# Clearing the zero rows of eight weight buffers on POOL in place of ScalarE copies, in a two-layer attention and MLP kernel

## The chip, the cores and the metric

The kernel runs on one core of a Trainium2 chip. The metric is the device time of one execution in microseconds (us). Before the change the median of three runs is 1509.63 us (1508.83 to 1510.06). The engines are named as the profile names them: PE is TensorE (PEld its weight loads), DVE is VectorE, ACT is ScalarE, POOL is GpSimd, and SP is SyncE, which issues all DMAs of this kernel.

## The reference

The input x has 2048 tokens of width 448. The program is two equal layers, each an attention with a recurrent memory followed by a gated MLP:

```python
def _A_ref(x, mem0, Wq, Wk, Wv, Wo, seg_len):      # 16 heads of 256, segments of 32, 8 memory rows
    mem = mem0
    for s in range(n_seg):
        h = concatenate([mem, x[:, s*32:(s+1)*32]])
        q, k, v = h @ Wq, h @ Wk, h @ Wv
        p = softmax(where(mask, q k^T * scale, -1e9))
        o = (p v) @ Wo
        mem = o[:, :8]                               # goes to the next segment
        outs.append(o[:, 8:])
def _B_ref(x, W_gate, W_up, W_down):
    gate = x @ W_gate
    return (relu(gate) * (x @ W_up)) @ W_down
x = x + _A_ref(_layernorm(x), mem0, ...)
x = x + _B_ref(_layernorm(x), ...)
x = x + _A_ref(_layernorm(x), mem0, ...)             # same weights again
x = x + _B_ref(_layernorm(x), ...)
```

All data are bfloat16. The two layers share all weights.

## The kernel before

The kernel first folds the attention weights. For each head it forms A = Wq Wk^T (scaled) and B = Wv Wo, both 448 wide, so that the 64 steps of the recurrence and all tokens use A and B and never q, k, v. For this it loads Wq, Wk and Wv in pieces of 512 columns (two heads) into 16 staging buffers `Wst`, each 128 partitions by 4 blocks by 512. Buffers 0 to 7 hold Wq and Wk in four groups (the even groups in 0 to 3, the odd ones in 4 to 7); buffers 8 to 15 hold Wv. Buffers 0 to 11 lie in `Bsb`, 12 to 15 in `glu`, and these are the names that the profile shows.

A weight has 448 rows: three blocks of 128 and one of 64. The fourth block of a staging buffer is therefore half filled, and its other half must be zero, since PE transposes whole blocks of 128 x 128 (`transposes`, profile line L745, eight matmuls for one head of one buffer). In buffers 0 to 7 the zero part is partitions 64 to 127, 512 columns. In buffers 8 to 15 it is two pieces of 64 partitions x 256 columns. The zeros are written once, in `constants`: by DVE for buffers 0 to 3 (L664), and for buffers 4 to 15 by ACT, which copies from a cleared tile `hG` (L666, which the profile shows under the helper's line L441). That is 4 copies of 64x512 and 16 of 64x256.

After a transpose, ACT or DVE evicts the block from PSUM into one of seven buffers `WT` (in `glu`; 128x896, lines L441 on ACT and L444 on DVE). Then `product` (L758) multiplies transposed Wq with transposed Wk, and the result goes to `A` (L441 on ACT, L443 on DVE). For a group PE transposes the first heads of four buffers, does 28 matmuls of products, and then the same for the second heads. In the first group the load of each buffer is split into halves (L706), so that the first heads arrive before the second ones. Later loads into the same buffers wait until PE has transposed the old contents.

Nothing of this is issued in program order. `_Sched` records every operation with its engine, a cost and its dependencies, and builds the order of each engine by simulating them: an engine takes, among the operations that can start at once, the one with the lowest step and priority. Each engine then works strictly in its order and waits on semaphores. Two things are fixed beside that. PE's order is written out by hand in the string `LINE`. And where PE would idle in the plan, `filler` puts in matmuls that compute nothing (L1403); at the very start PE also runs 17 matmuls on zeros (L657). POOL operations with the flag `cross` wait for POOL's own operation before and are waited for by the next one.

SP issues the weight loads, the loads of x (`X`), the first memory rows (`PTx`, ten small DMAs after POOL's memset L865), and later all else, also in one fixed order.

Of the kernel before, what the change touches and what calls it, by code (L numbers as in the profile page):

```python
# [423 lines left out]
def ev_cost(n, src="psum", fast=False):  # L424
    return {"act": 170 + 0.833 * n, "dve": 149 + (0.53 if fast else 1.04) * n, "pool": 170 + 1.0 * n}
# [10 lines left out]
def copy_any(out, in_, scale=None):  # L436

    def fn(E, eng):
        i = in_() if callable(in_) else in_
        if eng == "act":  # L440
            return E.activation(out, i, ACT.Copy, scale=1.0 if scale is None else scale)  # L441
        if scale is not None:
            return E.tensor_scalar(out, i, scale, None, op0=ALU.mult)  # L443
        return E.tensor_copy(out, i)  # L444
    return fn
# [66 lines left out]
class _Kernel:  # L512
# [124 lines left out]
    def constants(self):  # L637
        s = self.s
        iv = self.X[4][:, 0:256].bitcast(dt.int32)
        fv = self.X[5][:, 0:256].bitcast(F32)  # L640
        s.alias[("X", 4)] = ["ci"]
        s.alias[("X", 5)] = ["cf", "cf2"]

        def pool(fn, **k):
            s.add("pool", 500, lambda E, e: fn(E), **k)

        def dve(fn, **k):
            s.add("dve", 250, lambda E, e: fn(E), **k)

        hG = self.hG[0].rearrange("p a b -> p (a b)")  # L650
        hk = [("hG", 0, q) for q in range(2)]
        s.add("dve", 400, lambda E, e: E.memset(hG[:, 0:576], 0.0), w=hk)
        wb = self.bank("C")

        def spin(E, e):
            for _ in range(17):
                i = E.matmul(wb.ap()[:, 0:D], lhsT=hG[:, 0:128], rhs=hG[:, 128:576], start=True, stop=True)  # L657
            return i
        s.add("pe", 17 * 378, spin, r=hk, w=[wb], alloc=[wb])
        for i in range(16):  # L660
            for n, (rows, cols) in enumerate([(slice(64, 128), slice(0, 512))] if i < 8 else [(slice(64, 128), slice(0, 256)), (slice(0, 64), slice(256, 512))]):
                to, of = self.Wst[i][rows, 3, cols], hG[rows, cols]
                if i < 4:
                    s.add("dve", 300, lambda E, e, to=to: E.memset(to, 0.0), w=[("Wz", i, n)])  # L664
                else:
                    s.add("act", ev_cost(cols.stop - cols.start)["act"], copy_any(to, of), r=hk, w=[("Wz", i, n)])  # L666
        pool(lambda E: E.iota(iv[:, :], [[1, 128]], base=0, channel_multiplier=-1), w=["ci"])
        dve(lambda E: E.tensor_copy(fv[:, :], iv[:, :]), r=["ci"], w=["cf"])
        dve(lambda E: E.tensor_scalar(self.ident[:, :], fv[:, :], 0.0, None, op0=ALU.is_equal), r=["cf"], w=["ident"])
        dve(lambda E: E.memset(self.maskb[:, :], 0.0), w=["mask"])  # L670
        for b in range(4):
            q = slice(32 * b, 32 * b + 32)
            dve(lambda E, q=q, b=b: E.tensor_scalar(self.maskb[q, 0:SEG], fv[q, 0:SEG], -32.0 * b, FAR, op0=ALU.is_gt, op1=ALU.mult),
                r=["cf"], w=["mask"])

        dve(lambda E: E.tensor_reduce(fv[:, 0:32], self.ident[:, :].rearrange("p (j i) -> p i j", j=4), AX.X, ALU.add), r=["ident", "mask"], w=["cf"])
        dve(lambda E: E.tensor_copy(self.Sel[:, :], fv[:, 0:32]), r=["cf"], w=["Sel"])

        mb = self.bank("C")
        for o in range(4):  # L680
            dve(lambda E, o=o: E.tensor_copy(self.Usb[:, 128 * o:128 * o + 128].rearrange("p (h q) -> p h q", h=H),
                                             self.ident[:, 8 * o:8 * o + 8].unsqueeze(1).to_broadcast([128, H, 8])),
                r=["ident"], w=[("Usb", o)])
            s.add("pe", 30, lambda E, e, o=o: E.matmul(mb.ap()[:, L * o:L * o + L], lhsT=self.Usb[:, 128 * o:128 * o + 128],
                                                       rhs=self.maskb[:, :], start=True, stop=True),
                  r=[("Usb", o), "mask"], w=[mb], alloc=[mb] if o == 0 else ())
        dve(lambda E: E.tensor_copy(self.mask8[:, :, :], mb.ap()[:, 0:4 * L].rearrange("p (o k) -> p o k", o=4)), r=[mb], w=["mask8"])
        pool(lambda E: E.memset(self.Pr[:, :], 0.0), w=[("r", "P")])
        dve(lambda E: E.memset(self.cvec[:, 0:1], EPS), w=["cvec"])
        pool(lambda E: E.memset(self.YTm[:, :, :], 0.0), w=[("YTm", c) for c in range(2)] + [("YTr", c) for c in range(2)])  # L690
        pool(lambda E: E.memset(self.Pm[:, :], 0.0), w=[("m", "P")])
        for i in range(2):
            pool(lambda E, i=i: E.memset(self.xn[i][:, KZ:KT], 0.0), w=[("xnz", i)])
        pool(lambda E: E.memset(self.Usb[:, :], 0.0), w=[("Usb", r) for r in range(4)])
        pool(lambda E: E.memset(self.uT[:, 3], 0.0), w=[("uT2", a, b) for a in range(2) for b in range(2)])
        pool(lambda E: E.memset(self.mT[:, :, :], 0.0), w=MEM + ["mTr", "mT3"])
        for i in range(2):
            pool(lambda E, i=i: E.memset(self.Px[i][:, :, :], 0.0), w=[("Px", i)])
        for l in range(2):
            for i in range(NB[l]):  # L700
                for p in range(2):
                    pool(lambda E, l=l, i=i, p=p: E.memset(self.HR[l][i][p][:, KZ:KW], 0.0),
                         w=[k for h in range(2) for k in (("HRx", l, i, p, h), *(("HRm", l, 4 * i + 2 * p + h, v) for v in range(4)))])

    def dma(self, dst, src, nbytes, r=(), w=(), prio=None, land=None):
        return self.s.add("sp", 750 if nbytes < 8192 else 640, lambda E, e: E.dma_start(dst, src), r=r, w=w, dma=nbytes, prio=prio, land=land)  # L706
# [821 lines left out]
```

## Time and profile before

| | us |
|---|---|
| median of 3 runs | 1509.63 |
| range of the runs | 1508.83 to 1510.06 |
| the profiled execution: time | 1508.01 |
| the profiled execution: span of the trace | 1506.2 |
| PE busy in the span | 1489.1 (99%) |
| DVE busy | 1147.8 (76%) |
| ACT busy | 914.4 (61%) |
| POOL busy | 166.2 (11%) |

Times in the trace count from the start of the span; the execution's own time is 1.8 us longer. A row of the timeline has start, duration, engine, line, operation, what is written and read, the count, and in brackets how long the engine stood idle before and what ended that. A helper records most copies, so one line can stand for many tiles. "PE busy" says little by itself, as matmuls are pipelined; the granted clock (1.00 is full speed) and the waits say more.

### The profile page before, as it was taken

How to read it: one execution, taken by the hardware profiler on the slowest of the kernel's cores; microseconds unless marked ns; L12 is line 12 of the kernel's file. 1: busy time of each engine (PE TensorE's matmuls, PEld its weight loads, DVE VectorE, ACT ScalarE, POOL GpSimd, SP SyncE). 2: the span in 40 equal slices, each digit the busy share in tenths (PEclk: the TensorE clock that was granted, in tenths of full speed). 3: DMA queues.
4: the chain of work that ended last, by engine and by line, in shares of the span. 5: the costliest groups of instructions: out<-in, count | busy, mean ns of one | idle time of the engine just before them, and what ended most of it. 6: DMA issues, size and time to landing. Idle time of an engine off the chain costs nothing.

```text
span 1506.2 us, 83238 instructions
## 1 busy us (share of the span) xinstructions
PE 1489.1 (99%) x37022; PEld 1058.8 (70%) x37022; DVE 1147.8 (76%) x3561; ACT 914.4 (61%) x2535; POOL 166.2 (11%) x648
## 2 busy tenths in 40 slices
PE   8999999999999999999999999999999999999999
PEld 5657566666767777677768677677768776677776
DVE  5767678787877887787877877788787788787864
ACT  7776566665655666566665666556565566565643
POOL 1010111111111111010101111011110011010000
PEclk9999999999999999999999999999999999999999
DMA  6702100000000000000000000000000000000000
GB/s 194 219 24 67 52 8 12 11 9 8 9 4 9 14 8 14 4 16 6 14 8 9 14 9 15 3 17 6 18 5 8 13 9 14 5 8 8 12 8 12
DMA packets 62582, 34.12 MB, mean 23 GB/s; under 512 B 31872, under 2 KB 62096, under 8 KB 62224
## 3 DMA queue, kind: packets, MB, share of 16 engines
q1 hardware_dynamic: 62224, 28.80, 7.3%
q8 instruction: 292, 4.78, 1.3%
q14 instruction: 66, 0.54, 0.1%
HBM read 21.36 MB, written 1.84 MB: 15 GB/s over the span
## 4 chain that ended last, share of the span: by engine, by line
PE 95%; DVE 3%; ACT 2%; issue 0%; POOL 0%; DVEq 0%
PE psG L451 24%; PE psG L1271 17%; PE psG L1369 12%; PE psC L970 11%; PE psC L931 9%; PE psG L931 3%; PE psG L1182 3%; PE psG L758 3%; PE psG L1297 3%; PE psC L451 2%; PE psC L1182 1%; PE psC L1125 1%; PE psG L745 1%; PE psG L1185 1%; PE psC L1271 1%; PE psG L970 1%
## 5 line engine op out<-in xcount | busy, mean ns | idle before, releaser
L1271 PE MATMUL psG<-HT,A 64*128 64x128 bf16 x4968 | 285.3, 216 | 0.1
L451 PE MATMUL psG<-Bsb,YT 128*128 128x448 bf16 x1288 | 276.6, 352 | 0.0
L1271 PE MATMUL psG<-HX,A 64*128 64x128 bf16 x3726 | 266.6, 216 | 0.0
L1271 PEld LDWEIGHTS psG<-HT,A 64*128 64x128 bf16 x4968 | 233.8, 94 | 14.1 <-issue 5.7
L441 ACT ACTIVATE Ug<-psG 64x128 bf16<-64x128 f32 (+2 forms) x428 | 153.6, 378 | 67.9 <-PE psG L1271 59.0
L1271 PEld LDWEIGHTS psG<-HX,A 64*128 64x128 bf16 x3726 | 193.7, 94 | 0.4 <-issue 0.4
L1369 PE MATMUL psG<-G,glu 64*128 64x128 bf16 x5936 | 187.9, 216 | 0.4 <-DVE G L444 0.2
L1369 PEld LDWEIGHTS psG<-G,glu 64*128 64x128 bf16 x5936 | 174.1, 94 | 12.5 <-issue 5.7
L970 PE MATMUL psC<-Bsb,YTm 128*32 128x448 bf16 x3584 | 181.4, 353 | 1.0 <-DVE YTm L444 0.6
L451 PEld LDWEIGHTS psG<-Bsb,YT 128*128 128x128 bf16 x1288 | 112.5, 97 | 89.3 <-issue 5.9
L931 PE MATMUL psC<-A,mT 64*32 64x448 bf16 x3948 | 154.9, 350 | 1.4 <-ACT mT L441 0.5
L1109 DVE STREAM_TRANSPOSE uT<-Usb 128x384 bf16<-128x384 bf16 x280 | 154.0, 551 | 0.9
L931 PE MATMUL psG<-A,mT 64*32 64x448 bf16 x3892 | 152.2, 350 | 0.0
L970 PEld LDWEIGHTS psC<-Bsb,YTm 128*32 128x32 bf16 x3584 | 90.0, 97 | 73.3 <-DVE YTm L444 3.1
L441 ACT ACTIVATE YT<-psG 128x448 bf16<-128x448 f32 x238 | 120.6, 543 | 11.3 <-PE psG L1185 10.4
L444 DVE CAST Ug<-psG 64x128 bf16<-64x128 f32 (+2 forms) x274 | 112.8, 422 | 18.2 <-PE psG L1271 14.3
L931 PEld LDWEIGHTS psC<-A,mT 64*32 64x32 bf16 x3948 | 79.6, 92 | 58.2 <-ACT mT L441 5.9
L1374 ACT ACTIVATE hG<-psG 128x512 bf16<-128x512 f32 (+1 forms) x126 | 68.5, 544 | 65.3 <-PE psG L1369 61.4
L451 PE MATMUL psG<-glu,hG 128*128 128x448 bf16 x448 | 98.6, 352 | 0.0
L1375 DVE TENSOR_TENSOR hG<-hG,psG 128x512 bf16<-128x512 bf16 (+1 forms) x117 | 70.6, 609 | 32.6 <-ACT hG L1374 31.7
L976 ACT ACTIVATE Ohi<-psC 128x448 bf16<-128x448 f32 x66 | 35.9, 544 | 95.6 <-PE psC L970 94.2
L931 PEld LDWEIGHTS psG<-A,mT 64*32 64x32 bf16 x3892 | 79.8, 92 | 17.4 <-ACT mT L441 0.6
(241 smaller groups left out, 2891.1 us busy)
## 6 DMA issues: line engine op xcount, KB each, us to landing
HR<-xn SPq DMA_DIRECT2D x128, 32.0 KB
Tsb<-Rsb SPq DMA_DIRECT2D x256, 1.5 KB
Tsb<-Rsb SPq DMA_DIRECT2D x256, 2.0 KB
Bsb<-in_A_Wq_dram SPq DMA_DIRECT2D x6, 384.0 KB
Bsb<-in_A_Wk_dram SPq DMA_DIRECT2D x6, 384.0 KB
HR<-Rsb SPq DMA_DIRECT2D x126, 1.5 KB
HR<-Rsb SPq DMA_DIRECT2D x126, 2.0 KB
X<-in_A_x_dram SPq DMA_DIRECT2D x16, 112.0 KB
```

Of the source, the lines that this page charges most:

```text
L441: return E.activation(out, i, ACT.Copy, scale=1.0 if scale is None else scale)
L444: return E.tensor_copy(out, i)
L451: return E.matmul(out, lhsT=lhsT, rhs=rhs, **k)
L758: i = E.matmul(bk.ap()[row0:row0 + mn, 0:D], lhsT=lhs[:, et, m0:m0 + mn], rhs=rhs[:, et, :], start=(et == 0), stop=(et == 1), tile_positio ...
L931: i = E.matmul(ub[v].ap()[32 * j:32 * j + 32, 0:D], lhsT=self.mT[rw, WHERE[b], first:first + 32], rhs=cols, start=(b == 0), stop=(b == 6), ...
L970: x = E.matmul(bo.ap()[32 * j:32 * j + 32, 0:D], lhsT=self.YTm[:, q, :], rhs=self.Bsb[:, chunks[q], :], start=(i == 0), stop=(i == 13), ti ...
L1109: self.s.add("dve", 578, lambda E, e, out=out, hh=hh: E.transpose(out, heads[hh]), r=[("Usb", 2 * half + v) for v in range(2)], w=[f"uT{ha ...
L1182: return E.matmul(ps[:, n * q:n * q + n], lhsT=HR[rows, 128 * q:128 * q + 128], rhs=PT, start=True, stop=True, tile_position=(b, 0))
L1271: i = E.matmul(ub[v].ap()[:, 128 * n:128 * n + 128], lhsT=self.A[rw, b, a0:a0 + 128], rhs=HT[rw, WHOLE[b], :, 0:SEG] if CROSS[b] is None e ...
L1369: i_ = E.matmul(two[v].ap()[:, 128 * c:128 * c + 128], lhsT=self.Wgu[rw, b, f0:f0 + 128], rhs=G[rw, WHOLE[b] if CROSS[b] is None else 4 + ...
L1374: s.add("act", 170 + 0.833 * N, lambda E, e, dst=dst, z=two[0], N=N: E.activation(dst, z.ap()[:, 0:N], ACT.Relu), r=[two[0]], w=[("hG", i, ...
L1375: s.add("dve", dv_cost(N), lambda E, e, z=two[1], N=N, dst=dst: E.tensor_tensor(dst, dst, z.ap()[:, 0:N], ALU.mult), r=[two[1]], w=[("hG", ...
```

## The change

ACT's sixteen copies of 64x256, which clear buffers 8 to 15, are no longer made. In their place POOL clears the same pieces with sixteen memsets. These are recorded last in `constants`, behind POOL's other memsets there, each with the flag `cross`. Buffers 0 to 7 are cleared as before (DVE for 0 to 3, ACT for 4 to 7).

```diff
+        rest = []
         for i in range(16):
             for n, (rows, cols) in enumerate([(slice(64, 128), slice(0, 512))] if i < 8 else [(slice(64, 128), slice(0, 256)), (slice(0, 64), slice(256, 512))]):
                 to, of = self.Wst[i][rows, 3, cols], hG[rows, cols]
                 if i < 4:
                     s.add("dve", 300, lambda E, e, to=to: E.memset(to, 0.0), w=[("Wz", i, n)])
+                elif i < 8:
+                    s.add("act", ev_cost(cols.stop - cols.start)["act"], copy_any(to, of), r=hk, w=[("Wz", i, n)])
                 else:
-                    s.add("act", ev_cost(cols.stop - cols.start)["act"], copy_any(to, of), r=hk, w=[("Wz", i, n)])
+                    rest.append(lambda to=to, i=i, n=n: s.add("pool", 350, lambda E, e, to=to: E.memset(to, 0.0), w=[("Wz", i, n)], cross=True, at=10 + n))
...
+        for f in rest:
+            f()
```

In the built program the order of PE, DVE and SP is the same, instruction by instruction. ACT has the sixteen copies less and is otherwise in the same order. POOL has the sixteen memsets between the memsets of `HR` (L702) and that of `PTx` (L865), and is otherwise in the same order.

## The prediction

> **What bounds the kernel now.** I read the page first (the chain that ended last, by engine), then the waits of TensorE (PE), then the timeline of the first 45 us by engine, because the change touches only the set-up.
>
> ```profile
> PE 95%; DVE 3%; ACT 2%; issue 0%; POOL 0%; DVEq 0%
> ```
>
> ```profile
> PE psG L758 <- ACT glu L441: 4.3, 2, 4.1
> PE psC L451 <- DVE Olo L979: 1.4, 3, 0.6
> ```
>
> The first fence is the page: 95% of the chain is PE, whose order is fixed by hand. The second is the waits of PE over the whole span (us in all, times, longest). A saving on PE's stream should therefore reach the end of the run, and the largest wait that PE has anywhere, 4.1 us at once, is for ScalarE's (ACT's) eviction of a transposed weight. The timeline of ACT, PE, DVE and SP's queue shows where it is (start, us, instruction, idle before it):
>
> ```profile
> 2.02 5.56 ACT L441 ACTIVATE Bsb<-hG 64x512 bf16<-64x512 bf16 x12
> 7.61 3.48 ACT L441 ACTIVATE glu<-hG 64x256 bf16<-64x256 bf16 x8
> 11.00 1.70 ACT L441 ACTIVATE glu<-psG 128x896 bf16<-128x896 bf16 x2
> ```
>
> ```profile
> 6.05 2.26 PE L745 MATMUL psG<-ident,Bsb 128*128 128x128 bf16 x32
> 8.15 0.61 PE L1403 MATMUL psC<-ident 128*128 128x128 bf16 x8
> 12.84 1.71 PE L758 MATMUL psG<-glu 128*64 128x448 bf16 x8 [4.08 <-ACT glu L441]
> ```
>
> ```profile
> 8.35 0.62 DVE L444 COPY glu<-psG 128x896 bf16<-128x896 bf16 x1 [0.58 <-PE psG L745]
> ```
>
> ACT copies zeros without a pause from 2.02 to 11.0 us and only then evicts two of the four transposed blocks that PE made between 6.05 and 8.3. DVE's two were done at 8.35 + 0.62 = 8.97. So PE stands from 8.76 to 12.84, and the only cause is ACT's queue of zero copies. What follows on PE, in the chain of waits (start, us, what):
>
> ```profile
> 14.54 0.75 PE psC L1403 x6
> 15.29 1.71 PE psG L745 x16
> 17.00 2.60 PE psG L758 x19
> 19.60 1.01 PE psG L745 x16
> 20.61 0.02 issue
> 20.63 0.64 DVE glu L444
> 21.27 0.04 issue
> 21.31 2.46 PE psG L758 x24
> ```
>
> Sixteen transposes (L745) take 1.71 us here and 1.01 us a little later: the pause is paid for twice. The table by windows (length, busy of PE, PEld, DVE, ACT and POOL, then granted clock, DMA share, GB/s) shows why:
>
> ```profile
> 11.20:11.40 0.20, 0.00 (x0) 0.00 (x0) 0.00 (x0) 0.20 (x1) 0.00 (x0) 0.82 0.40 113
> 18.00:18.20 0.20, 0.20 (x4) 0.15 (x2) 0.00 (x0) 0.20 (x1) 0.00 (x0) 0.61 0.23 77
> 7.92:11.33 3.41, 0.84 (x15) 0.66 (x12) 0.62 (x1) 3.24 (x9) 0.00 (x0) 1.00 0.71 200
> 11.33:14.74 3.41, 1.91 (x11) 0.91 (x12) 0.16 (x1) 1.91 (x3) 0.00 (x0) 0.50 0.85 247
> 14.74:18.15 3.41, 3.41 (x30) 2.63 (x29) 1.09 (x2) 1.14 (x2) 0.00 (x0) 0.50 0.93 290
> ```
>
> The clock falls from 1.00 to 0.50 at about 11.33 (0.82 is the mean of that slice) and returns at about 18.15.
>
> **The change part by part.** *ACT.* Sixteen zero copies of 64x256 leave; four of 64x512 stay. Eight cost 3.48, or 0.435 each; the row of twelve (four large, eight small) leaves 5.56 - 3.48 = 2.08 for the large ones, so ACT is free at 4.1 instead of 11.0. Its two evictions (1.70 / 2 = 0.85 each) then start as the first and third blocks come, and end by about 8.8, before DVE's second at 8.97. That copy is late next: from a copy's start to PE's the chain shows 0.64 + 0.04 (20.63 to 21.31), so PE starts L758 at 8.35 + 0.68 = 9.03. Gain at this point: 12.84 - 9.03 = 3.81.
>
> *The clock.* PE's pause falls from 4.08 to about 0.3 us, so I take the clock to stay at 1.00. Then, by full-speed rows: eight L758 at 2.46 / 24 each are 0.82 (to 9.85), six fillers L1403 at 0.61 / 8 each 0.46 (to 10.31).
>
> *A load is late next.* The following transposes need the second half of a third weight buffer, the seventh load that SP issues. SP does not wait for anybody here, so this load does not come earlier:
>
> ```profile
> 4.20 1.13 SPq L706 DMA_DIRECT2D Bsb<-in_A_Wk_dram  x2
> 5.37 1.13 SPq L706 DMA_DIRECT2D Bsb<-in_A_Wq_dram  x2
> 6.54 1.14 SPq L706 DMA_DIRECT2D Bsb<-in_A_Wk_dram  x2
> 7.72 1.13 SPq L706 DMA_DIRECT2D Bsb<-in_A_Wq_dram  x2
> ```
>
> ```profile
> 7.24 0.90 PEld L745 LDWEIGHTS psG<-ident,Bsb 128*128 128x128 bf16 x16 [0.31 <-DMA Bsb<-in_A_Wk_dram]
> ```
>
> The fourth load, issued at 4.20, released PE's weight load at 7.24, 3.04 later. The seventh, issued at 7.72, would release it at 10.76, and the matmul about 0.1 behind: 10.85. So PE waits some 0.5 us for DMA. From there at full speed: 16 transposes 1.01, twenty L758 2.05, 16 transposes 1.01, and 0.70 from 20.61 to 21.31: the L758 that started at 21.31 starts at 15.62. **Sum: 21.31 - 15.62 = 5.7 us.** With no wait for that load it would be 6.2.
>
> *Behind that.* The order of PE, DVE and SP is untouched, and the loads of the next group wait on SP for PE's transposes, so they move forward with PE. The four loads of the second group, which wait for nobody, do not move; the last ends at about 18.0 (in the slice from 18.00 the DMA share falls to 0.23). Its transposes are in
>
> ```profile
> 25.30 1.71 PE L745 MATMUL psG<-ident,Bsb 128*128 128x128 bf16 x24
> ```
>
> and would come at 25.30 - 5.7 = 19.6: a margin of 1.6 us. I keep 5.7 to the end of the run.
>
> *POOL.* Sixteen memsets of 64x256, each waiting for POOL's own instruction before, stand between the HR and PTx memsets (POOL's timeline, and SP's row for the first user of PTx):
>
> ```profile
> 4.17 0.64 POOL L698 MEMSET Px<- 128x256 bf16 x2
> 4.76 2.24 POOL L702 MEMSET HR<- 128x192 bf16 x10
> 6.95 0.31 POOL L865 MEMSET PTx<- 128x256 bf16 x1
> ...
> 63.07 0.64 POOL L444 COPY uT<-tl 64x128 bf16<-64x128 bf16 x2 [1.36 <-DVE tl L1102]
> ```
>
> ```profile
> 25.12 2.23 SPq L706 DMA_DIRECT2D PTx<-in_A_mem_dram  x6
> ```
>
> Unwaited memsets cost 0.22 (HR) to 0.32 (Px); two waiting copies add about 0.06 between them (0.64 for two of 0.29). I take 0.40: 6.4 us, from 7.0 to 13.4, and PTx's memset ends at 13.8. SP's DMA into PTx, at 25.12 - 5.7 = 19.4, waits for it, with SP's later loads behind it. So POOL costs nothing up to (19.4 - 0.4 - 7.0) / 16 = 0.75 each. The cleared buffers hold the value weights, which are not even asked for until
>
> ```profile
> 34.42 1.12 SPq L706 DMA_DIRECT2D Bsb<-in_A_Wv_dram  x2
> ```
>
> *DVE beside POOL.* The trace shows the same short copy at 0.57 and at 0.22, both beside memsets of POOL:
>
> ```profile
> 3.16 0.57 DVE L681 COPY Usb<-ident 128x128 bf16<-128x128 bf16 x1
> ...
> 5.35 0.22 DVE L681 COPY Usb<-ident 128x128 bf16<-128x128 bf16 x1
> ```
>
> So each of DVE's evictions from 7 to 13 us could cost 0 to 0.35 more. On the path lie the copies that end at 8.97; two of them cost 0.7 at most, of which the wait for the load hides 0.5. I take 0 and keep 0.2 for the range. The Trainium skill, "SBUF — State Buffer", section "Who interferes with whom", has DVE and GpSimd exclude each other only where DVE works in a two-port mode or reads two SBUF operands; an eviction from PSUM is neither, and by it the term is 0 too. No row of this trace shows such an eviction wholly beside a memset.
>
> The profiled execution took 1508.01 us, 1.6 below the median of 1509.63 shown; on it the change gives 1502.3, on the median **1503.9**.
>
> **The rivals.**
>
> *The clock falls all the same.* The window from 7.92 to 11.33 had 0.84 us of PE and the clock fell at its end; in the changed kernel it would hold 0.84 + 0.82 + 0.46 + 0.5 = 2.6 of 3.41. For it: 1.91 of 3.41 did not bring the clock back. Against: it is three times as full as the window that lost it. If it falls for one such window, half of 3.41 is lost, 1.7 us: 1505.6; for two, 1507.3. The Trainium skill, "TensorE: Matmul & The Clock Gate", Part 1, describes a free-running window of about 3.4 us that grants or takes the clock by activity. The trace agrees on the length: 18.15 - 11.33 is twice 3.41. Part 4 adds that transposes do not count as activity in the same way; by that the window would hold only 1.9 of 3.41, which no row here can exclude.
>
> *The gain is taken up later* by transfers that cannot start sooner. From 14.74 to 18.15 the DMA share is 0.93, and the next loads would join that queue at once. If they cost PE half the gain, 1506.8. Against: no DMA is among PE's longer waits.
>
> *Nothing is gained:* if PE's real wait at 12.84 were for something else. ACT ran without a gap up to its release, so I hardly believe it: 1509.6.
>
> *Slower: POOL holds up SP.* If clearing 64 partitions at a time is dear on POOL, PTx's memset comes late, and SP's DMA into PTx stands in front of the loads of the fourth group. It passes today's place of 25.12 from (25.12 - 0.4 - 7.0) / 16 = 1.1 us a memset. At 1.6 each it would end at 33.0, 7.9 later than today; if none of that is slack, 1517.5. Against: the short memsets of the trace cost 0.32 or less, on 128 partitions.
>
> **How the numbers follow.** Forecast as summed: 0.70, with 1503.2 to 1504.9 as its own range (0.5 for the load, 0.2 for DVE, and the 1.2 us that the three runs of before are apart). Clock falls: 0.11. Gain taken up: 0.10. Nothing: 0.05. Slower: 0.04. A measurement here tells about 0.2%, or 3 us: faster means below 1506.6. The first case, most of the second and half of the third are faster: 0.85; within 0.2%: 0.11; slower: 0.04. The range goes from 1502.8 (all loads in time, 6.2, less run spread) to 1506.8, which takes in both middle cases.
>
> **What would show it.** ACT's evictions start before 7 us; the first L758 starts near 9.0; the granted clock is 1.00 from 7.9 to 18.2; PE waits about 0.5 for Wq at 10.8; the L758 row of 21.31 stands near 15.6; POOL's memsets end by 14; the same shift of 5.7 at 60 us and at the end. Wrong, if the clock dips, if a DMA wait over 1 us appears on PE before 45 us, or if the shift shrinks between 60 us and the end.

## The result, and the profile after

| | before | after |
|---|---|---|
| median of the runs on the same chip, us | 1508.83 (1507.65 to 1510.23, 9 runs) | 1504.3 (1503.03 to 1506.16, 9 runs) |
| ratio of the times, 95% interval | | 0.9972 (0.9961 to 0.9982) |
| profiled execution: time, span, us | 1508.01, 1506.2 | 1504.3, 1501.8 |
| mean granted clock of TensorE | 0.998 | 1.000 |

The forecast was 1503.9 us, 5.7 below the median it started from. The kernel became faster by 4.5 us against the runs beside it. A second comparison (first experiment) gives 5.5.

First the waits of TensorE over the whole span of the changed kernel (us in all, times, longest):

```profile
PE psC L451 <- DVE Olo L984: 1.4, 3, 0.6
PE psC L657 <- DVE hG L652: 1.2, 1, 1.2
PE psG L763 <- DVE glu L444: 1.0, 4, 0.3
```

The wait of 4.1 us for ScalarE, the largest before, is no longer among them. Every wait over 0.3 us that is left was there before (the one for DVE's evictions has grown from 0.7 to 1.0 us in all), and a wait of 0.2 us for a weight load is new. (Lines from 706 on stand 5 further down in this kernel: L745 is now L750, L758 is L763, L1403 is L1408, L706 is L711.)

The timeline of the first 35 us of the changed kernel, by engine (start, us, instruction, idle before it):

```profile
2.03 2.18 ACT L441 ACTIVATE Bsb<-hG 64x512 bf16<-64x512 bf16 x4
7.37 1.81 ACT L441 ACTIVATE glu<-psG 128x896 bf16<-128x896 bf16 x2 [3.17 <-PE psG L750]
```

```profile
7.07 2.85 POOL L669 MEMSET Bsb<- 64x256 bf16 x8
9.97 2.85 POOL L669 MEMSET glu<- 64x256 bf16 x8
12.88 0.32 POOL L870 MEMSET PTx<- 128x256 bf16 x1
```

```profile
7.82 0.62 DVE L444 COPY glu<-psG 128x896 bf16<-128x896 bf16 x1 [1.61 <-PE psG L750]
8.71 0.62 DVE L444 COPY glu<-psG 128x896 bf16<-128x896 bf16 x1 [0.27 <-PE psG L750]
```

```profile
1.22 5.67 PE L657 MATMUL psC<-hG 128*128 128x448 bf16 x17 [1.22 <-DVE hG L652]
6.73 1.95 PE L750 MATMUL psG<-ident,Bsb 128*128 128x128 bf16 x32
8.51 0.61 PE L1408 MATMUL psC<-ident 128*128 128x128 bf16 x8
9.39 0.95 PE L763 MATMUL psG<-glu 128*64 128x448 bf16 x8 [0.27 <-DVE glu L444]
10.27 0.51 PE L1408 MATMUL psC<-ident 128*128 128x128 bf16 x6
10.96 1.07 PE L750 MATMUL psG<-ident,Bsb 128*128 128x128 bf16 x16 [0.18 <-DMA Bsb<-in_A_Wq_dram]
```

ScalarE stands idle for 3.17 us before its first eviction, so it is no longer what is late. POOL clears the sixteen halves while PE transposes. DVE's copies take 0.62 beside these memsets, as they did without them. PE starts L763 at 9.39 where it started at 12.84. After these products and six fillers it waits 0.18 us for the weight load, to 10.96. The chain that ended last, from there on (start, us, what):

```profile
8.35 2.56 DMA Bsb<-in_A_Wq_dram
...
10.96 1.07 PE psG L750 x16
12.02 2.01 PE psG L763 x20
14.04 1.01 PE psG L750 x16
...
15.75 2.46 PE psG L763 x24
```

The sixteen transposes that took 1.71 us take 1.07, and the L763 that started at 21.31 starts at 15.75: 5.56 us earlier. The part up to this row is called the head below. The same three windows as before (length, busy of PE, PEld, DVE, ACT and POOL with their counts, then granted clock, DMA share, GB/s):

```profile
7.92:11.33 3.41, 2.96 (x43) 2.11 (x41) 1.78 (x3) 1.81 (x3) 2.89 (x10) 1.00 0.74 200
11.33:14.74 3.41, 3.41 (x47) 2.34 (x45) 1.87 (x3) 2.67 (x5) 1.58 (x6) 1.00 0.85 251
14.74:18.15 3.41, 3.14 (x39) 1.85 (x36) 1.87 (x3) 2.17 (x4) 0.00 (x0) 1.00 1.02 298
```

The clock stays at 1.00 in all three, where it was 0.50 in the last two.

How the shift (start of a matmul in the first trace of before less its start in the other trace, matmuls taken in order, median of 15; times are those of before) goes on behind the head, with three further executions that the experiments gave:

| at, us | 22 | 60 | 650 | 990 | 1200 | end |
|---|---|---|---|---|---|---|
| after | 5.56 | 5.55 | 5.9 | 6.2 | 5.3 | 4.44 |
| after, second execution | 5.55 | 5.25 | 4.9 | 4.7 | 4.5 | 4.74 |
| after with two loads exchanged | 5.53 | 5.03 | 5.6 | 5.9 | 5.9 | 6.01 |
| before, second execution | 0.90 | 0.90 | 1.8 | 2.2 | 1.8 | 1.54 |

Behind 60 us it moves by -1.1 to +1.0 in steps of 0.2 to 0.4, and it moves as much between two executions of the kernel before. One step, at 995 us (-0.30), is the same in the first row and in the last, so that one belongs to the first trace of before.

### The profile page after: what moved, and what is told of

The parts are those of the page before. It is cut to its first block, busy times and chain, and to the rows that moved or that the text cites. A ratio compares the mean times of both kernels' runs of the same rounds, so it can differ in the third digit from the quotient of the medians.

```text
span 1501.8 us, 83238 instructions
## 1 busy us (share of the span) xinstructions
PE 1487.6 (99%) x37022; PEld 1057.6 (70%) x37022; DVE 1148.6 (76%) x3561; ACT 908.3 (60%) x2519; POOL 171.8 (11%) x664
## 4 chain that ended last, share of the span: by engine, by line
PE 95%; DVE 3%; ACT 1%; SPq 0%; issue 0%; DMA 0%; POOL 0%; DVEq 0%
PE psG L451 24%; PE psG L1276 17%; PE psG L1374 12%; PE psC L975 11%; PE psC L936 9%; PE psG L936 3%; PE psG L1187 3%; PE psG L763 3%; PE psG L1302 3%; PE psC L451 2%; PE psC L1187 1%; PE psC L1130 1%; PE psG L750 1%; PE psG L1190 1%; PE psC L1276 1%; PE psG L975 1%
```

## The experiments

The theory: the ScalarE queue is the wait; the gain is a shorter pause plus a clock that no longer falls, cut off by the next weight load; nothing behind the head belongs to the change. The rivals: the clock term is worth nothing by the end; POOL has a price that shows only later; the pause is not ScalarE's.

**1. The changed kernel again.** Same code, to see which steps behind the head recur.

> The changed kernel once more, for a second trace. In the first one the head of the kernel is 5.56 us earlier than in the profile of before, and the end 4.44 us. If the missing 1.1 us are scatter of single executions (short stops of PE at places that differ from run to run), a second trace shows the head within 0.2 us of the first one and the end anywhere from 4 to 6 us ahead, with the steps between 60 us and the end at other places. If the change itself loses the 1.1 us further on, the steps stand at the same places again (near 995, 1032, 1167, 1334 to 1390 and 1468 us). Time: 1503 to 1506.

It took 1504.29 us (1503.27 to 1506.69, 5 runs), ratio 0.9968 (0.9955 to 0.9981), beside a before of 1509.75 (1507.48 to 1512.23, 23 runs). The end of the head and the clock are the same; at 17.9 us one eviction of ScalarE came late for PE and took 0.3 off the shift. The steps behind 60 us stand at other places and sizes than in the first execution (second row of the table). I therefore take the loss of 1.1 us behind 60 us in the first trace as scatter of single executions; a small true loss inside that scatter isn't excluded, since the shift shrank in both traces (5.55 to 4.44 and 5.25 to 4.74).

The head of this execution tests the terms of the forecast better than the first one. The 17 opening matmuls took 5.05 us, nearly as in the first trace of before (4.99), and its timeline reads

```profile
9.14 0.95 PE L763 MATMUL psG<-glu 128*64 128x448 bf16 x8 [0.27 <-DVE glu L444]
10.96 1.07 PE L750 MATMUL psG<-ident,Bsb 128*128 128x128 bf16 x16 [0.43 <-DMA Bsb<-in_A_Wq_dram]
```

PE comes 0.25 us sooner than in the first execution and waits that much longer: the load lets it go at 10.96 in both.

**2. The pause filled, ScalarE's work left as it was.** Kernel before, with 58 more filler matmuls in PE's pause, so that only the clock is changed.

```diff
 # filler(), for the first filler only
+        self.nf = getattr(self, 'nf', 0) + 1
+        if self.nf == 1:
+            n += 58
```

> The kernel before with 58 more idle matmuls of PE (L1403) in its pause behind the first transposes, so that the pause lasts under 1 us, while ACT's zero copies and all else stay. My theory: the first L758 still starts at about 12.8 (it waits for ACT), but the clock stays at 1.00, and the L758 that started at 21.31 starts at 12.84 + 0.82 + 0.46 + 1.01 + 2.05 + 1.01 + 0.70 = 18.9: 2.4 us gained, 1507 for a median of 1509. The rival, that the slow stretch behind the pause comes from loads or evictions and not from the clock: it stays at 21.3 and the time at 1509.

The chain shows the clock term as expected, at the head:

```profile
12.84 0.95 PE psG L761 x8
13.79 0.44 PE psC L1406 x6
14.23 0.89 PE psG L748 x16
```

The eight L761 took 0.95 where they took 1.71 at half clock, the first L761 of the 24 starts 2.45 us earlier than before, and the granted clock is 1.000. But the kernel took 1511.83 us (1510.39 to 1513.17, 10 runs), ratio 1.0013 (1.0003 to 1.0022): slower. The profiled execution was the slowest of the ten. Its span of 1511.4 ends 5.2 later than before's, so 7.6 us went behind the head in it; by the medians, 2.1 apart, it is about 4. The waits of PE name no engine for it:

```profile
PE psG L934 <- issue: 2.3, 4, 1.1
PE psG L1274 <- issue: 2.0, 4, 0.8
```

"issue" is time in which the engine waited for nothing that the profile shows. The largest such stop is a piece of the chain at 134.69:

```profile
134.69 1.14 issue
```

So the run told two things at once, and its total tells nothing of the clock. Two more kernels (5 and 9) take them apart.

**3 and 4. Smaller doses.** The changed kernel with four, then six, of the eight buffers given back to ScalarE.

```diff
-                elif i < 8:
+                elif i < 12:     # dose 8: POOL clears buffers 12 to 15
+                elif i < 14:     # dose 4: POOL clears buffers 14 and 15
```

> Half of the change: POOL clears buffers 12 to 15 only (eight memsets), ACT keeps the eight copies into Bsb. ACT would be free at 7.6, evicts from 7.6 to 9.3, and PE's first L758 starts at 9.45, nearly as in the changed kernel (9.39 there), because DVE's second copy ends at 9.3 anyway; then the load holds PE to 10.9. So the whole gain with half of the change: within 0.3 us of the changed kernel at 16 us, 1504 to 1505. The rival, that ACT's freed time counts by the copy (7 us of copies for 5.6 us of gain): half the gain, 2.8 us, 1506 to 1507.

> A quarter of the change: POOL clears buffers 14 and 15 only (four memsets). ACT is free at 11.0 - 4 x 0.435 = 9.3, evicts to 11.0, the first L758 starts at 11.1, and PE pauses 2.3 us. The load is no longer waited for. If a pause of this length leaves the clock at 1.00, the L758 of 15.75 starts at 17.1, a gain of 4.2 against before: 1505 for 1509. If the clock falls, one window of 3.41 us costs 1.7 and two 2.5 as in before: 18.8 to 19.6, 1506.5 to 1507.3. The half dose beside it says whether the gain falls off only here.

With eight halves moved: 1505.76 us (1504.02 to 1507.27, 7 runs), ratio 0.9974 (0.9963 to 0.9984); 1504 to 1505 was expected. The shift at the head is 5.38, nearly that of all sixteen: beyond eight, ScalarE is not what is late. Then a load of the second group is, in the chain:

```profile
13.04 6.12 DMA Bsb<-in_A_Wq_dram
...
19.25 0.61 PE psG L750 x8
```

The transposes came at the load, and the shift at 60 us is 4.46. PE waits 0.9 us for this load here and 0.4 in run 6; in the changed kernel its transposes start at 18.14 without a wait.

With four halves moved: 1507.07 us (1505.75 to 1509.01, 10 runs), ratio 0.9984 (0.9975 to 0.9994). The pause is half as long, and the clock holds at 1.00 (timeline, windows and chain of this kernel):

```profile
11.09 0.95 PE L763 MATMUL psG<-glu 128*64 128x448 bf16 x8 [2.01 <-ACT glu L441]
```

```profile
7.52:10.94 3.42, 1.51 (x24) 1.34 (x24) 0.68 (x2) 3.32 (x7) 1.14 (x4) 1.00 0.72 194
```

```profile
17.10 2.46 PE psG L763 x24
```

PE starts L763 at 11.09 for 12.84, 1.75 earlier, but the head's shift is 21.31 - 17.10 = 4.21: the other 2.46 is the clock, as in run 2 (2.45). A window with 1.51 us of PE in 3.42 kept it, the one with 0.84 in 3.41 lost it. Both hold the eight fillers (0.61), and the rest is transposes. That fits transposes counting as activity, but these two windows don't prove it: the pause was also shorter (2.01 for 4.08). Run 7 has a window that does: from 44.05 to 47.46 (its windows counted in steps of 3.41 from the rise of its clock at 6.50) PE was busy for 2.15 us, 2.01 of them transposes (the row is of these alone), and the clock stayed at 1.00:

```profile
44.05:47.46 3.41, 2.01 (x32) 1.66 (x30) 1.00 0.87 253
```

Without its transposes it would have held 0.14 us, less than any window here that lost the clock, and stood empty from 44.05 to 46.80.

On this chip the medians gain 2.7, 4.0 and 5.5 us with 4, 8 and 16 halves moved, for 4.21, 5.38 and 5.56 at the head. The order is that of the heads, though the intervals overlap. The two small doses have 1.4 to 1.5 less at the end. The wait for the load explains a part for eight (0.9), and stops of PE put down to issue another: they come to 1.3 us in the trace with four, 0.8 with eight and 0.3 with sixteen. The rest is open.

**5. The place in the stream alone.** Kernel before, with the 17 opening matmuls of 448 columns cut into 75 of 102: 58 instructions more, the same columns, nothing else.

```diff
-            for _ in range(17):
-                i = E.matmul(wb.ap()[:, 0:D], lhsT=hG[:, 0:128], rhs=hG[:, 128:576], start=True, stop=True)
+            for _ in range(75):
+                i = E.matmul(wb.ap()[:, 0:102], lhsT=hG[:, 0:128], rhs=hG[:, 128:230], start=True, stop=True)
```

> A control for the fillers. With 58 more idle matmuls the head was 2.45 us earlier and the end 5.2 us later than before: 7.6 us went in stops of PE behind 60 us, which the profile puts down to issue. Here the kernel before gets the same 58 more matmuls without any time: the first spin on zeros (L657) is 75 matmuls of 102 columns in place of 17 of 448 (7650 columns for 7616). If the place of PE's later instructions in its stream is what makes the stops, the head is as before (L758 at 12.8 and 21.3) and the end 6 to 8 us later than before, with stops at the same matmuls as with the fillers: 1515 to 1517. If the stops came from the fillers or from the time at which the rest runs, the time is that of before, 1509 to 1510.

It took 1511.74 us (1510.23 to 1512.75, 7 runs) beside a before of 1508.2 (1505.69 to 1509.44, 19 runs), ratio 1.0024 (1.0013 to 1.0035). At the head it is 0.23 behind, at the end 3.7: 3.5 us were lost between, again to

```profile
PE psG L1271 <- issue: 0.9, 2, 0.6
PE psG L931 <- issue: 0.8, 1, 0.8
```

The stops stand at the same matmuls of before's order as in run 2 for a part: at 135.7 us (-1.13 here, -1.50 there), 387.8 (-0.48, -0.46), 938.3 (-0.55, -0.55), 1303.3 (-0.44, -0.80). Others of run 2, at 116.2 and 323.1, have none here. The loss was half of what was expected.

**6. Two loads exchanged.** The changed kernel with SP's fifth and seventh load exchanged, so that the load PE waits for at 10.96 comes 2.3 us sooner.

```diff
+        sp = [k for k, o in enumerate(seq) if o.eng == "sp"]
+        for k in (8, 9):
+            p, q = sp[k], sp[k + 4]
+            seq[p], seq[q] = seq[q], seq[p]
+            seq[p].seq, seq[q].seq = p, q
```

> The changed kernel with two loads of SP exchanged: the second half of the third buffer is issued fifth in place of seventh (and that of the first buffer seventh). PE's wait for a load at 10.9 goes; its transposes start when the six fillers end, near 10.8, and the L758 of 15.75 starts at 15.5 to 15.6. The load of 12.4 (third buffer of the second group), for which PE waited 0 to 0.9 us in three traces, is then next to hold it, at about 18. So 0 to 0.2 us in all: the same as the changed kernel within what can be measured. The rival, that the seventh load cost more than the 0.2 us of the trace: over 0.5 us at 16 us.

It took 1502.92 us (1501.96 to 1505.95, 7 runs), ratio 0.997 (0.9959 to 0.9981): not told apart from the changed kernel. At the head nothing is won (5.53), but this doesn't show what the load is worth: the 17 opening matmuls took 6.04 us in this execution (5.67 in the changed kernel's first), and PE came to the transposes only at 11.00, without a wait. PE then waits for a load of the second group to 18.68, as with eight halves.

**7. POOL made late.** The changed kernel with eleven more memsets of 128x1792 on POOL between the sixteen and PTx's, to put a number on the rival "slower".

```diff
+        for i in range(11):
+            s.add("pool", 61, lambda E, e: E.memset(self.YTm[:, :, :], 0.0), cross=True, at=10,
+                  w=[(k, c) for k in ("YTm", "YTr") for c in range(2)] if i == 10 else [])
```

> The changed kernel with eleven more memsets of 128x1792 on POOL between the sixteen and that of PTx; they clear again what is zero already. They cost 1.65 each, 18 us, so PTx's memset ends near 31.4 in place of 13.2, and SP's DMA into PTx, at 20.7 in the changed kernel, waits about 10.7 us, with the loads of the fourth group behind it (25.15 to 33.8). My theory: cover is worth what the loads have in hand. The first of them is needed at 35.5 and would be there at about 37.3, the others a little later: 2 to 4 us lost, 1506 to 1508. If all of the delay reaches PE: 8.5 us, 1513. If nothing does: 1504.

It took 1509.12 us (1508.81 to 1511.25, 10 runs), ratio to before 1.0013 (1.0003 to 1.0022). Timelines of POOL and of SP's queue:

```profile
12.88 18.11 POOL L710 MEMSET YTm<- 128x1792 bf16 x11
31.04 0.31 POOL L873 MEMSET PTx<- 128x256 bf16 x1
```

```profile
31.38 2.06 SPq L714 DMA_DIRECT2D PTx<-in_A_mem_dram  x6
33.48 0.93 SPq L714 DMA_DIRECT2D Bsb<-in_A_Wk_dram  x2
```

In the changed kernel, without the eleven, the same queue reads

```profile
20.68 2.23 SPq L711 DMA_DIRECT2D PTx<-in_A_mem_dram  x6
25.15 0.93 SPq L711 DMA_DIRECT2D Bsb<-in_A_Wk_dram  x2
```

The shift is 5.59 at 22 us and 5.35 at 30. SP then stands at PTx's DMA 10.7 us longer, the loads queued behind it come late, and between 30 and 50 us the shift falls from 5.35 to -0.73: 6.1 us, more than expected. The rival's mechanism is real. Its deciding point was put too low: here the DMA is issued 6.3 us later than in the kernel before (31.38 against 25.12) and PE loses 0.7 to before, so some 5.5 us of that are slack. The sixteen memsets would have to fill POOL from 7.07 to about 31, 1.5 us each, before the gain is gone; they take 0.36.

**8. The kernel before again**, one execution.

> The kernel before once more, for a second trace, to see how much two executions of one kernel differ behind the head: steps of 0.1 to 0.4 us at some twenty places if the scatter is that of single executions, the head the same within 0.1 us if the clock falls and rises at the same distance from PE's pause. The clock's windows need not stand at the same times, so the slow stretch could be one window long in place of two: then the L758 of 21.3 stands near 20.

One execution, 1506.46 us, span 1504.7. The windows, of 3.41 us, stand elsewhere:

```profile
9.80:13.21 3.41, 0.37 (x4) 0.31 (x6) 0.00 (x0) 2.85 (x5) 0.00 (x0) 1.00 0.77 221
13.21:16.62 3.41, 3.41 (x31) 2.50 (x26) 0.63 (x1) 1.30 (x2) 0.00 (x0) 0.50 0.89 275
16.62:18.00 1.38, 1.38 (x17) 0.85 (x18) 1.03 (x2) 0.73 (x3) 0.00 (x0) 1.00 0.99 308
```

The pause again takes the clock, but for one window instead of two, and the head is 0.9 us earlier than in the first trace. What the clock costs the kernel before is thus not one number; against the 18.86 at which run 2 starts its 24 L761 from the same pause, it is 21.31 - 18.86 = 2.45 us in the first trace and 20.41 - 18.86 = 1.55 in this one.

**9. The pause filled with no instruction more.** Kernel before; the first filler is 14 matmuls of 512 columns in place of 8 of 128, and the second filler of 6 is left out. The count of PE's instructions is that of before.

```diff
 # filler()
+        if self.nf == 1:
+            n, ns = 14, 0
+        if self.nf == 2:
+            return None
 # what the first one issues
+            if ns == 0:
+                for _ in range(n):
+                    i = E.matmul(self.psum[bank][:, :], lhsT=w, rhs=w.unsqueeze(1).to_broadcast([128, 4, 128]), start=True, stop=True)
+                return i
```

> The fillers again, now without moving anything in PE's stream: the first filler is 14 matmuls of 512 columns in place of 8 of 128, and the second filler (6 of 128) is left out, so that PE's count of instructions is that of before. PE is busy to about 11.2 and pauses 1.6 us; ACT and all else as before. The clock stays at 1.00; the first L758 starts at 12.8 still, and the one of 21.31 at 12.84 + 0.82 + 1.01 + 2.05 + 1.01 + 0.70 = 18.4, 2.9 earlier than in the first trace of before (2.0 earlier than in the second, where the slow stretch was one window). If the 58 fillers lost their gain by displacing PE's stream, the head's gain now reaches the end: 2 to 2.9 us faster than before. If fillers or an early head cost something of their own, it is again slower than before by 2 us.

It took 1507.2 us (1505.53 to 1508.08, 11 runs) beside a before of 1508.85 (1506.83 to 1512.08, 21 runs), ratio 0.9985 (0.9976 to 0.9993). Its chain:

```profile
12.84 0.95 PE psG L764 x8
13.79 1.00 PE psG L751 x16
...
18.52 2.46 PE psG L764 x24
```

PE starts at 12.84 as in the kernel before, since ScalarE is as late as ever; from there all is at full clock, and the head is 2.79 us earlier, of which 0.44 is the second filler. With the count of the stream unchanged, the kernel is faster over the runs: 1.65 us in the medians (2 to 2.9 was expected), 1.1 to 3.6 by the interval, which is more than the 0.44 of the filler. The profiled execution itself doesn't show it at its end (span 1506.2, as before), since it has 2.2 us of stops put down to issue at L1277. So such stops come without a displaced stream too.

**10. Both together.** The changed kernel with the 58 instructions of run 5 (the same edit).

> The changed kernel with the first spin split into 75 matmuls of 102 columns, as in the control on the kernel before: 58 more matmuls in PE's stream and no more time in them. The control lost 3.5 us by it (1.0024 against before). If the stops hang on the place of PE's instructions in the stream and not on when they run, the changed kernel loses the same 3.5 us and stands near 1507.5, ratio to before about 0.9993; the stops are at the same matmuls as in the control. If they hang on the time, they are elsewhere and the loss is another one.

It took 1510.14 us (1508.37 to 1511.85, 10 runs), ratio 1.0009 (1.0000 to 1.0019). The head is 4.84 us earlier than before, the end 1.39 later: 6.2 us lost, where 3.5 was expected. Many of the stops stand at sites of runs 2 or 5 (116.2 us, 323.1, 387.8, 938.3, 1303.3), but not all: the largest of both, at 135.7, is missing, and one of 0.9 us at 461.8 is in neither. Again they have no releaser:

```profile
PE psG L1276 <- issue: 1.6, 4, 0.6
PE psG L936 <- issue: 1.5, 2, 0.9
```

A gain of 4.5 to 5.5 us (measured on other chips) was thus turned into a loss by instructions that take no time themselves.

What these stops wait for can be seen in the records of DMA transfers, which the waits do not use. One queue carries instructions (292 transfers and 4.78 MB in the trace of before). In run 2 one of them, from 132.99 to 134.26, stands just before the stop that lasts from 134.69 to 135.84 (DMA of 132.9 to 134.3):

```profile
q8 instruction: 1, 0.02, 5.7%
```

PE goes on 1.57 us after the transfer's end. The twelve traces hold 48 stops of over 0.15 us that are put down to issue, and every one of them ends 1.23 to 1.60 us after the end of such a transfer, though there are some 4.5 us from one transfer to the next and just 8% of all matmuls start 1.2 to 1.6 us after one. So these stops are tied to the bringing in of instructions; no run changed that by itself. They come to 5.2, 3.0 and 3.9 us in the three displaced traces (runs 2, 5 and 10), 2.2 in run 9, and 0 to 1.3 in the other eight. That isn't all that was lost: the traces of runs 2, 5 and 10 lose 7.6, 3.5 and 6.2 us behind the head. Why the same 58 cost 3.5 us in run 5 by the medians, about 4 in run 2 and about 6 in run 10 stays open.

## Why the prediction was right

- *What waits.* Right. ScalarE was free at 2.03 + 2.18 = 4.21 (4.1 forecast), its evictions ended at 7.37 + 1.81 = 9.18 (8.8), and DVE's copy was late next. They were to start before 7 us; they started at 7.37, and at 6.76 in the second execution. The dose runs show that ScalarE's queue sets the pause: 4.08 with none moved, 2.01 with four.
- *First L758.* 9.39 and not 9.03. The 17 opening matmuls took 5.67 us here and 4.99 in the trace of before, because the clock rose later after the start (at 5.88 for 4.50; over the executions here the opening takes 4.80 to 6.04). The wait for the load hid this. In the second execution, with an opening of 5.05, it was 9.14.
- *The clock.* Right: 1.00 throughout the head. Runs 2, 4 and 9 show the term there (2.3 to 2.5 us against the first trace of before, about 0.9 less against the second), and run 9 shows it in the medians. The rival's window of 7.92 to 11.33 was not one in this execution: counted from the rise at 5.88, one runs from 9.29 to 12.71, and PE was busy for 3.14 us of it. Two rules of the Trainium skill bear on this rival, "TensorE: Matmul & The Clock Gate". Part 1, "The HAM clock gate", has a free-running window that does not reset when a kernel starts: the traces agree, since the rise moves by over a microsecond between executions and the slow stretch is one window or two (3.41 or 6.82 us). Part 4, "PE-mode transpose", would not have transposes count as activity in the same way: here the traces speak against it (the window of run 7 shown with run 4).
- *A load is late next.* Right: 10.96 against 10.85. PE waited 0.18 us for it, and 0.43 in the second execution (0.5 forecast). Both executions go on at 10.96 whether PE comes early or late, so this load sets the head's gain. How much more an earlier load would give isn't shown: run 6 meant to tell, and its slow opening covers it.
- *POOL.* Right: 0.36 us from memset to memset (2.85 / 8) for the 0.40 taken, PTx's memset done at 13.2 for 13.8, and 7.5 us ahead of the DMA that needs it. The deciding point for the rival was 1.5 us a memset (run 7), not 1.1: the prediction counted none of the delay as slack.
- *DVE beside POOL.* Right at 0: 0.62 with and without.
- *"I keep 5.7 to the end of the run".* The head's 5.7 was 5.56. At the end the profiled execution had 4.44, its second one 4.74, the version with two loads exchanged 6.01; the medians say 4.5 and 5.5. The prediction named a shift that shrinks between 60 us and the end as a sign of being wrong, and by that sign this step failed in both traces of the changed kernel. As the shift grew instead in the version with two loads exchanged, and moved as much between two executions of before, the step was good only to about 1 us. That 1504.3 came so near to 1503.9 is in part luck: the base moved too, from 1509.63 to 1508.83, and the gain was 4.5 or 5.5 for 5.7.
- *The margin of 1.6 us* was misread. What ends at about 18.0 is not the last load of the second group. By their semaphores in the trace of before, the third load (issued at 12.40) is complete at 18.02 and the last at 19.11. And the transposes that wait for the third are not those of 25.30 but those of 23.70, which would come at 23.70 - 5.7 = 18.0, as the chain with eight halves shows, where they wait for it. So there was no margin. In the changed kernel the load is complete at 17.99 and the transposes start at 18.14; with eight halves moved and in runs 6 and 7 PE waits 0.9, 0.4 and 0.2 us for it. That it cost nothing in the profiled execution of the change is luck by 0.15 us.

## What to carry to other kernels

A pause of PE is to be priced twice: its length, and the windows of half clock that follow it if the window around it is mostly empty; even halving the pause can save the second part whole. Then ask what is late next, because that caps the gain: eight moved halves were worth as much at the head as sixteen. And when an edit changes the number of PE's instructions, compare with a kernel that has the same number: 58 matmuls that add no time of their own cost 3.5 to 6 us of 1509, as much as the whole change won.

## What was not expected of the hardware

- PE stops without a releaser at particular matmuls ("issue", 0.15 to 1.1 us each), and all 48 such stops of the traces end 1.2 to 1.6 us after a transfer of instructions. With 58 matmuls more before them the stops come to 3.0 to 5.2 us, otherwise to 0 to 2.2; three sites (387.8, 938.3 and 1303.3 us) stop in all three kernels that have the displacement, others in one or two.
- The clock's windows of 3.41 us lie differently to the start of each execution, so the same pause costs one slow window or two.
- A window with PE busy for 1.51 of 3.42 us keeps the full clock; 0.84 of 3.41 and 0.37 of 3.41 lose it. Transposes count in this (run 7). The last window of the changed kernel, with 1.32 of 3.41, loses it as well (the clock is 0.50 from 1500.92), so if the busy share is what decides, the line lies between 1.32 and 1.51; the length of the pause (1.9 us and less kept, about 2.1 and more lost, within a window) would sort these windows as well.
